# Scoring the last three groups a group ahead, and mixing two quarters directly, in a fused attention and two-FFN kernel

## The chip, the cores and the metric

The kernel runs on one core of a Trainium2 chip. The metric is the device time of one execution in microseconds, as the median of several runs. The engines are TensorE (PE; its weight loads are shown as PEld), VectorE (DVE), ScalarE (ACT), GpSimd (POOL) and SyncE (SP), which here only issues DMAs. Each engine takes its instructions in the order in which the program lists them.

## The reference

12480 tokens of 128 numbers attend to 32 inducing points, and the result goes through two feed-forward layers of width 2048.

```python
def mab(q, kv):
    s = scale * (q @ kv.transpose(0, 2, 1))
    s = s - s.max(-1, keepdims=True)
    a = np.exp(s)
    a /= a.sum(-1, keepdims=True) + 1e-09
    return a @ kv
h = mab(I, x)                      # 32 points attend to 12480 tokens
y = mab(x, h)                      # 12480 tokens attend to 32 points
# first layer
u = y @ w_in
y = (u * np.clip(u + 3.0, 0.0, 6.0) / 6.0) @ w_out
# second layer
r = np.maximum(y @ w_in2, 0.0)
out = (r * r) @ w_out2
```

The four weight matrices are float64 in memory, read as 64-bit words and turned into float32 on the chip.

## The kernel before

**The first pass** (lines 420 to 442) computes `h`. The tokens come in eight groups (`GROUPS`, of 2, 4, 4, 4, 4, 3, 2 and 2 blocks, each block four times 128 or 48 tokens). For group g, `scores` makes the 32 scores of each token on TensorE (L339, 256, 304 or 512 columns) and their running maximum on VectorE (L343); `exps` makes the exponentials on ScalarE (L349); `turn_x` transposes the tokens (L359) and copies them out (ScalarE, L364); `turn_e` transposes the exponentials (L372) and copies them out (VectorE, L374, and L377 for a block of 48); `accumulate` multiplies the two (L384, copy L388). In iteration g, group g is scored and its tokens are turned, while the exponentials of group g-1 are turned and accumulated. The scores use two PSUM buffers, the transposes four, the exponentials two. After the last group, `common_max` and `weigh` (L393 to L417) weigh the groups against each other, and lines 443 to 466 sum them and divide, which gives `ht4`, four copies of the transposed `h`.

**Weights are converted beside it.** A matrix is handled in quarters, a0 to a3 for the first up projection, b for its down projection, c and d for the second layer. A quarter has three steps: `first_stage` (ScalarE L179; VectorE L187, L191), `second_stage` (VectorE L200, L208) and `third_stage` (an add on GpSimd, L220). `tick()` puts the steps of `EARLY` between the others: tick 8 and 9 belong to iteration 4, 10 and 11 to iteration 5, and so on. `third_stage` of a quarter frees its load buffer, and once all loads of `LOADS` are out it also issues the next loads, c0 first (L156); the first to do so is that of b1, in `beside(-1, ...)` ahead of the main loop.

**Loads** are issued by SyncE in the order of `LOADS`: x is a group of tokens, a and b are quarters, n is the copy of the last group that needs no transpose.

**Mixing.** The tokens' second attention and the first up projection are merged: `a_t` (attention weights, `att_turn`, L641) times `m4`, where `m4` is `h` times the first weight matrix, as a high and a low part. `m4` has 128 rows: two copies of the 32 high rows and two of the low ones. Quarter 0 of its columns is made directly from `ht4` (`mix`, L484, 128 rows at once; `mix_high`, L490; `mix_low`, L494). Quarters 1 to 3 are made for 32 rows each (`mix_rest`, L501), split by `rest_high` (L516) and `rest_low` (L522), and spread to their rows by DMAs (`spread_rest`, L509, 64 KB each). `fill` issues transposes whose result nobody reads.

**The main loop** (k = 0 to 199 and a tail) runs `up1(k)` (L679, two matmuls of quarter k // 2 for the first eight k), `gate1(k)` (ScalarE L687, VectorE L688), `down1(k - 2)` (L715) and, 11 steps later, the second layer. The PSUM tag `h` has three buffers that `ps`, `rest`, `pt`, `h1` and `h2` take in turn; `y` and `o` have one each. The second block of 512 tokens gets its attention weights from `att_scores(1)` at k = 2 to `att_turn(1)` at k = 5, where the tile `pt` is written.

Of the kernel before, what the change touches and what calls it, by code (L numbers as in the profile page):

```python
# [30 lines left out]
KEPT = 5  # L31
TURN_V = {}
NATURAL = {7}


LOADS = [("x", 0), ("x", 1), ("x", 2), ("a", 0), ("x", 3), ("a", 1), ("x", 4), ("a", 2), ("a", 3),
         ("x", 5), ("b", 0), ("x", 6), ("x", 7), ("b", 1), ("n", 7), ("b", 2), ("b", 3)]

# [30 lines left out]
def induced_attention_then_two_ffn(  # L71
# [185 lines left out]
    def fill(n, pool, tag, bufs):  # L257
        t = pool.tile([P, P], F32, tag=tag, name="fill", bufs=bufs)
        for i in range(n):
            nc.tensor.transpose(t, ident, ident)  # L260
# [3 lines left out]
    def tick():  # L264
        ticks.append(len(ticks))
        return jobs(EARLY.get(ticks[-1], ""))
# [3 lines left out]
    def load_until(item):  # L270
        while item in todo:
            load(todo.pop(0))
# [9 lines left out]
    with ExitStack() as pro:  # L282
# [52 lines left out]
        def scores(g):  # L335
            n = run[g]
            s1[g] = pps.tile([P, n], F32, tag="s1", name="s1", bufs=2)
            for j in range(J):
                nc.tensor.matmul(  # L339
                    s1[g][M * j:M * (j + 1), :], lhsT=inds, rhs=xg[g][:, j * n:(j + 1) * n],  # L340
                    start=True, stop=True,
                )
            nc.vector.tensor_reduce(  # L343
                out=nmax[:, g:g + 1], in_=s1[g], axis=AX.X, op=ALU.max, negate=True
            )

        def exps(g):
            es[g] = pp.tile([P, run[g]], F32, tag="es", name="es", bufs=2)
            nc.scalar.activation(  # L349
                es[g], s1[g], AF.Exp, bias=nmax[:, g:g + 1], scale=1.0,  # L350
                accum_out=lsum[:, g:g + 1],
            )
# [13 lines left out]
        def turn_e(g):  # L366
            nb = len(GROUPS[g])
            t = pps.tile([P, nb, P], F32, tag="xt", name="ett", bufs=4)
            et[g] = pp.tile([P, nb, P], F32, tag="et", name="et", bufs=2)
            for b, blk in enumerate(GROUPS[g]):  # L370
                o = sum(GROUPS[g][:b])
                nc.tensor.transpose(t[:blk, b, :], es[g][:, o:o + blk], ident)  # L372
            whole_blocks = sum(blk == P for blk in GROUPS[g])
            nc.vector.tensor_copy(et[g][:, :whole_blocks], t[:, :whole_blocks])  # L374
            for b in range(whole_blocks, nb):
                blk = GROUPS[g][b]
                nc.vector.tensor_copy(et[g][:blk, b], t[:blk, b])  # L377

        def accumulate(g):
            nb = len(GROUPS[g])  # L380
            acc = hacc[g % 2][:, g // 2, :]
            for b, blk in enumerate(GROUPS[g]):
                for j in range(J):
                    nc.tensor.matmul(  # L384
                        acc[M * j:M * (j + 1), :], lhsT=et[g][:blk, b, M * j:M * (j + 1)],
                        rhs=xn[g][:blk, j * nb + b, :], start=(b == 0), stop=(b == nb - 1),
                    )
            nc.scalar.copy(hsb[:, g, :], acc)  # L388


        def common_max():
            nmin = pp.tile([P, 1], F32, name="nmin")
            nc.vector.tensor_reduce(out=nmin, in_=nmax, axis=AX.X, op=ALU.min)  # L393
            nm4 = pp.tile([P, J], F32, name="nm4")
            nc.vector.tensor_scalar_mul(nm4, blk4, nmin)
            return nm4
# [23 lines left out]
        for g in range(NG):  # L420
            load_until(("x", min(g + 3, NG - 1)))
            load_until(("n", g))
            scores(g)
            if g:
                turn_e(g - 1)
            if g == NG - 1:
                load_until(todo[-1] if todo else None)
                nm4 = common_max()
            for b in range(len(GROUPS[g])):
                if g not in NATURAL:  # L430
                    turn_x(g, b)
                if b == 0:
                    exps(g)
            tick()
            if g:
                accumulate(g - 1)
            tick()
        turn_e(NG - 1)
        rw, rl = weigh(nm4)
        accumulate(NG - 1)  # L440
        tick()

        pg = pps.tile([P, D], F32, tag="xt", name="pg", bufs=4)
        for g in range(NG - 1):
# [4 lines left out]
            )  # L449
        hg = pp.tile([P, D], F32, tag="sel4", name="hg")  # L450
        nc.scalar.copy(hg, pg)
        pl = pps.tile([P, M], F32, tag="s1", name="pl", bufs=2)
        nc.tensor.matmul(pl, lhsT=ones, rhs=rl, start=True, stop=True)
        ph = pps.tile([P, M], F32, tag="xt", name="ph", bufs=4)
# [25 lines left out]
    mixed = {}  # L480

    def mix(q):
        mixed[q] = ap_.tile([P, CW], F32, tag="o", name="mixed")
        nc.tensor.matmul(  # L484
            mixed[q], lhsT=ht4.rearrange("p j i -> p (j i)"), rhs=whole.pop(("a", q)),
            start=True, stop=True,
        )

    def mix_high(q):
        nc.scalar.copy(m4[:, q * CW:(q + 1) * CW], mixed[q])  # L490
# [6 lines left out]

    def mix_rest():
        rest["m"] = hp.tile([P, CW], F32, tag="h", name="rest")
        for q in range(1, J):  # L500
            nc.tensor.matmul(  # L501
                rest["m"][M * (q - 1):M * q, :], lhsT=ht4[:, 0, :], rhs=whole.pop(("a", q)),
                start=True, stop=True,
            )

    def spread_rest(part, groups):
        for q in range(1, J):
            for i in groups:
                nc.sync.dma_start(  # L509
                    m4[M * i:M * (i + 1), q * CW:(q + 1) * CW].bitcast(F32),  # L510
                    part[M * (q - 1):M * q, :].bitcast(F32),
                )

    def rest_high():
        rest["h"] = ep.tile([P, CW], F32R, tag="hi1", name="resthigh")
        nc.scalar.copy(rest["h"][:M * (J - 1), :], rest["m"][:M * (J - 1), :])  # L516
        spread_rest(rest["h"], (0, 1))

    def rest_low():
        n = M * (J - 1)  # L520
        t = ep.tile([P, CW], F32R, tag="lo1", name="restlow")
        nc.vector.tensor_tensor(  # L522
            out=t[:n, :], in0=rest["m"][:n, :], in1=rest["h"][:n, :], op=ALU.subtract
        )
        spread_rest(t, (2, 3))
# [91 lines left out]
    def att_norm(c):  # L617
        a = att_weights(c)
        att[c] = a
        if c < TURNS:  # L620
            a4 = sp.tile([P, J, 2, 2, M], F32R, tag="a4", name="a4", bufs=1)
            nc.vector.tensor_copy(a4[:, :, 0, 0, :], a)
            nc.scalar.copy(a4[:, :, 1, 0, :], a)
            for u in range(2):
                nc.vector.tensor_tensor(
                    out=a4[:, :, u, 1, :], in0=a, in1=a4[:, :, 0, 0, :], op=ALU.subtract
                )
            att[c] = a4
            return a4[:, 0, 1, 1, :1].bitcast(F32)
        return a[:, 0, :1]  # L630
# [201 lines left out]
    mix(0)  # L832
    att_exp(0)
    mix_high(0)
    mix_rest()
    fill(8, ap_, "y", 1)
    att_norm(0)
    rest_high()
    att_turn(0)
    fill(3, ap_, "y", 1)  # L840
    mix_low(0)
    rest_low()
    merge(("b", 1))
    tick()
    beside(-1, tick())
# [1 line left out]
    for k in range(K + OFF + L2 + 1):  # L847
        c, p = divmod(k, NP)
        j = k - OFF

        if k == NP + L1 - 1:
            on(down1, k - L1)
        on(up1, k)
        on(gate1, k)
        if k < 2:
            fill(8, ap_, "o", 1)
        on(square2, j - 1)
        on(up2, j)
        on(relu2, j)
        on(high2, j - 1)  # L860
        on(low2, j - 2)
        on(low1, k - 1)
        if k != NP + L1 - 1:
            on(down1, k - L1)
        on(down2, j - L2)
        last = g1[k][:, 0, :1] if k < N1 else lo1[k - 1][:, 0, :1].bitcast(F32) if N1 < k < K else None
        last = jobs(LATER.get(k, "")) or last
        if c + 1 < NCH:
            for chunks in BATCHES[1:]:
                if p == 1 and c + 2 == chunks[0]:  # L870
                    load_x(chunks[:2])
                    load_x(chunks[2:])
            stage = p - 2 if c == 0 else p
            if stage == 0:
                att_scores(c + 1)
                last = att_shift(c + 1)
            if stage == 1:
                att_exp(c + 1)
            if stage == 2:
                last = att_norm(c + 1)  # L880
            if stage == 3:
                if c + 1 < TURNS:
                    att_turn(c + 1)
                else:
                    last = att_spread(c + 1)
        beside(k, last)
        on(high1, k)
# [28 lines left out]
```

## Time and profile before

| | us |
|---|---|
| median of 3 runs | 959.04 |
| lowest and highest run | 958.35, 960.85 |
| the profiled execution | 958.2 |
| its span, first to last instruction | 956.4 |

The page gives for each engine its busy time, its share of the span and its number of instructions. In the timeline a row is a run of like instructions of one engine: start, duration, engine, line, operation, written and read tiles, shapes, count, and in brackets how long the engine was idle before it and what ended that. `SPq` rows are the issuing of DMAs. The durations of matmuls are modelled and overlap.

### The profile page before, as it was taken

The page shows a single profiled execution, that of the slowest core. Times are in us where ns is not written, and L with a number is a line of the kernel's source. Part 1 is how long each engine was busy: PE and PEld are TensorE (multiplying, and loading weights), DVE is VectorE, ACT ScalarE, POOL GpSimd, SP SyncE. Part 2 cuts the span into 40 slices and gives each one's busy share as a digit, 9 for nine tenths or more (in the row PEclk, how much of TensorE's full clock was granted, in tenths as well). Part 3 has the DMA queues.
Part 4 walks back from the last instruction along what each step waited for, and adds up shares of the span by engine and source line. Part 5 has one row for each costly group of instructions (what it writes and reads, how often), then busy time and mean ns, then how long its engine had stood idle before and what let it go on. Part 6 is the DMA issues. An engine that isn't in the chain of part 4 may idle for free.

```text
span 956.4 us, 12916 instructions
## 1 busy us (share of the span) xinstructions
PE 944.8 (99%) x4617; PEld 767.1 (80%) x4617; DVE 794.2 (83%) x969; ACT 812.3 (85%) x925; POOL 248.6 (26%) x412
## 2 busy tenths in 40 slices
PE   9899999999999999999999999999999999999998
PEld 7546678888888888888888888888888888888898
DVE  5887788888888888888888888888888888888774
ACT  6568888888888888888888888888888888889887
POOL 1233222222222222222222222222222222222222
PEclk9999999999999999999999999999999999999999
DMA  9451000001000000100000100010000100000000
GB/s 365 150 184 56 7 18 23 2 21 38 31 22 18 5 23 16 52 23 10 14 23 9 47 23 8 17 56 6 18 23 4 45 23 3 21 20 2 17 13 15
DMA packets 31247, 35.07 MB, mean 37 GB/s; under 512 B 7632, under 2 KB 24272, under 8 KB 30672
## 3 DMA queue, kind: packets, MB, share of 16 engines
q1 hardware_dynamic: 31184, 34.25, 10.9%
q8 instruction: 36, 0.59, 0.2%
q14 instruction: 27, 0.22, 0.1%
HBM read 21.18 MB, written 6.39 MB: 29 GB/s over the span
## 4 chain that ended last, share of the span: by engine, by line
PE 95%; DVE 2%; DMA 1%; ACT 0%; SPq 0%; issue 0%; DVEq 0%; ACTq 0%
PE h L756 28%; PE oacc L727 27%; PE yacc L727 26%; PE h L679 9%; PE yacc L715 2%; PE oacc L715 1%; PE ps L543 1%; DMA xg<-in_xT 1%; PE xt L359 1%; DMA raw<-in_w2a 0%; PE s L339 0%; PE hacc L384 0%; SPq L509 0%; DVE cve L191 0%; DVE et L374 0%
## 5 line engine op out<-in xcount | busy, mean ns | idle before, releaser
L688 DVE SCALAR_TENSOR_TENSOR g<-g,h 128x1024 f32<-128x1024 f32 (+2 forms) x200 | 238.7, 1193 | 119.2 <-ACT g L687 116.7
L687 ACT ACTIVATE g<-h,small 128x1024 f32<-128x1024 f32 (+2 forms) x200 | 219.1, 1096 | 114.4 <-PE h L679 114.1
L791 DVE TENSOR_TENSOR lo<-g,hi 128x1024 fp32r<-128x1024 f32 (+3 forms) x193 | 229.3, 1189 | 7.8 <-PE oacc L727 4.1
L707 DVE TENSOR_TENSOR lo<-g,hi 128x1024 fp32r<-128x1024 f32 (+2 forms) x184 | 219.4, 1192 | 0.8 <-POOL hi L699 0.8
L771 ACT ACTIVATE g<-g 128x1024 f32<-128x1024 f32 (+3 forms) x201 | 206.0, 1025 | 0.2
L767 ACT ACTIVATE g<-h 128x1024 f32<-128x1024 f32 (+3 forms) x201 | 199.2, 992 | 3.3 <-PE h L756 2.1
L783 ACT CAST hi<-g 128x1024 fp32r<-128x1024 f32 (+1 forms) x186 | 191.7, 1031 | 0.0
L699 POOL TENSOR_SCALAR hi<-g 128x1024 fp32r<-128x1024 f32 (+2 forms) x182 | 187.3, 1029 | 0.4 <-DMA at<-al 0.2
L756 PE MATMUL h<-yh,wl 128*128 128x512 f32 (+2 forms) x400 | 153.7, 384 | 0.0
L756 PE MATMUL h<-yh,wh 128*128 128x512 f32 (+2 forms) x400 | 153.7, 384 | 0.0
L756 PE MATMUL h<-yl,wh 128*128 128x512 f32 (+2 forms) x400 | 153.7, 384 | 0.0
L679 PE MATMUL h<-at,m 128*128 128x512 f32 (+2 forms) x400 | 129.0, 404 | 2.5 <-DMA m<-restlow 2.1
L727 PE MATMUL oacc<-hi,wh 128*128 128x512 f32 (+2 forms) x384 | 116.5, 384 | 0.0
L727 PE MATMUL oacc<-hi,wl 128*128 128x512 f32 (+2 forms) x384 | 116.4, 384 | 0.0
L727 PE MATMUL oacc<-lo,wh 128*128 128x512 f32 (+2 forms) x384 | 116.4, 384 | 0.0
L826 POOL COPY small<-lo 128x1 f32<-128x1 f32 x115 | 21.7, 189 | 344.5 <-DVE lo L707 344.5
L727 PE MATMUL yacc<-hi,wl 128*128 128x512 f32 (+2 forms) x368 | 111.2, 383 | 0.0
L727 PE MATMUL yacc<-hi,wh 128*128 128x512 f32 (+2 forms) x368 | 111.2, 383 | 0.0
L727 PE MATMUL yacc<-lo,wh 128*128 128x512 f32 (+2 forms) x368 | 111.2, 383 | 0.0
L679 PEld LDWEIGHTS h<-at,m 128*128 128x128 f32 x400 | 74.3, 188 | 26.0 <-issue 8.5
L756 PEld LDWEIGHTS h<-yl,wh 128*128 128x128 f32 x400 | 75.1, 188 | 14.5
L756 PEld LDWEIGHTS h<-yh,wh 128*128 128x128 f32 x400 | 75.1, 188 | 14.2
(125 smaller groups left out, 915.5 us busy)
## 6 DMA issues: line engine op xcount, KB each, us to landing
outT<-osb SPq DMA_DIRECT2D x23, 256.0 KB, 2.2
xc<-in_xT SPq DMA_DIRECT2D x9, 512.0 KB, 4.6
xg<-in_xT SPq DMA_DIRECT2D x4, 1024.0 KB, 7.2
at<-ah SPq DMA_DIRECT2D x168, 16.0 KB, 1.8
at<-al SPq DMA_DIRECT2D x168, 16.0 KB, 1.8
raw<-in_w1a SPq DMA_DIRECT2D x4, 512.0 KB, 8.7
raw<-in_w1b SPq DMA_DIRECT2D x4, 512.0 KB, 7.1
raw<-in_w2a SPq DMA_DIRECT2D x4, 512.0 KB, 6.3
```

The source lines that it names most:

```text
L679: nc.tensor.matmul(h1[k][:, u, :size[c]], lhsT=m4[:, f * P:(f + 1) * P], rhs=a_t[c], start=True, stop=True)
L687: nc.scalar.activation(g1[k], h, AF.Relu, bias=three)
L688: nc.vector.scalar_tensor_tensor(out=g1[k], in0=g1[k], scalar=6.0, in1=h, op0=ALU.min, op1=ALU.mult)
L699: nc.gpsimd.tensor_scalar(out=hi1[k], in0=g1[k], scalar1=1.0, scalar2=1.0, op0=ALU.mult, op1=ALU.mult)
L707: nc.vector.tensor_tensor(out=lo1[k], in0=g1.pop(k), in1=hi1[k], op=ALU.subtract)
L715: nc.tensor.matmul(acc, lhsT=w[:, f * P:(f + 1) * P], rhs=g[:, u, :], start=(p == 0 and u == 0), stop=(p == NP - 1 and u == 1),)
L727: nc.tensor.matmul(acc, lhsT=w[:, f * P:(f + 1) * P], rhs=g[:, u, :], start=(p == 0 and n == 0), stop=(p == NP - 1 and n == 5),)
L756: nc.tensor.matmul(h2[k][:, u, :size[c]], lhsT=w, rhs=y, start=(n == 0), stop=(n == 2))
L767: nc.scalar.activation(g2[k][:, u, :], h[:, u, :n], AF.Relu)
L771: nc.scalar.activation(g2[k][:, u, :], g2[k][:, u, :], AF.Square)
L783: nc.scalar.copy(hi2[k][:, u, :], g2[k][:, u, :])
L791: nc.vector.tensor_tensor(out=lo2[k][:, u, :], in0=g[:, u, :], in1=hi2[k][:, u, :], op=ALU.subtract)
```

## The change

The order of the first pass is changed for groups 5, 6 and 7. They are scored, and their exponentials made, at the end of the iteration before theirs, behind `turn_x` of that iteration and ahead of its first tick. In the last iteration, which then has no scores, `common_max` comes first, the exponentials of groups 6 and 7 are turned one behind the other, `weigh` follows, and two fill transposes stand ahead of `accumulate(6)`. The tick with the first step of b1 comes after the copy `hg`. In `LOADS`, x5 goes ahead of a3 and x6 ahead of b0.

In the mixing, quarters 0 and 1 are made directly (`mix(1)` in the PSUM buffer `y`), and quarters 2 and 3 go through `mix_rest` and the DMAs, of which there are now four for the high part and four for the low. Eight fill transposes go. `rest_high` moves behind the low parts of the direct quarters, and `rest_low` moves into the main loop, behind `gate1(0)`.

```diff
@@ -31,10 +31,11 @@
 KEPT = 5
 TURN_V = {}
 NATURAL = {7}
-
-
-LOADS = [("x", 0), ("x", 1), ("x", 2), ("a", 0), ("x", 3), ("a", 1), ("x", 4), ("a", 2), ("a", 3),
-         ("x", 5), ("b", 0), ("x", 6), ("x", 7), ("b", 1), ("n", 7), ("b", 2), ("b", 3)]
+AHEAD = 5
+
+
+LOADS = [("x", 0), ("x", 1), ("x", 2), ("a", 0), ("x", 3), ("a", 1), ("x", 4), ("a", 2), ("x", 5),
+         ("a", 3), ("x", 6), ("b", 0), ("x", 7), ("b", 1), ("n", 7), ("b", 2), ("b", 3)]
 
 
 
@@ -420,25 +421,31 @@
         for g in range(NG):
             load_until(("x", min(g + 3, NG - 1)))
             load_until(("n", g))
-            scores(g)
+            if g < AHEAD:
+                scores(g)
+            if g == NG - 1:
+                load_until(todo[-1] if todo else None)
+                nm4 = common_max()
             if g:
                 turn_e(g - 1)
             if g == NG - 1:
-                load_until(todo[-1] if todo else None)
-                nm4 = common_max()
+                turn_e(g)
+                rw, rl = weigh(nm4)
             for b in range(len(GROUPS[g])):
                 if g not in NATURAL:
                     turn_x(g, b)
-                if b == 0:
+                if b == 0 and g < AHEAD:
                     exps(g)
+            if AHEAD <= g + 1 < NG:
+                scores(g + 1)
+                exps(g + 1)
             tick()
             if g:
+                if g == NG - 1:
+                    fill(2, pps, "xt", 4)
                 accumulate(g - 1)
             tick()
-        turn_e(NG - 1)
-        rw, rl = weigh(nm4)
         accumulate(NG - 1)
-        tick()
 
         pg = pps.tile([P, D], F32, tag="xt", name="pg", bufs=4)
         for g in range(NG - 1):
@@ -449,6 +456,7 @@
             )
         hg = pp.tile([P, D], F32, tag="sel4", name="hg")
         nc.scalar.copy(hg, pg)
+        tick()
         pl = pps.tile([P, M], F32, tag="s1", name="pl", bufs=2)
         nc.tensor.matmul(pl, lhsT=ones, rhs=rl, start=True, stop=True)
         ph = pps.tile([P, M], F32, tag="xt", name="ph", bufs=4)
@@ -480,7 +488,7 @@
     mixed = {}
 
     def mix(q):
-        mixed[q] = ap_.tile([P, CW], F32, tag="o", name="mixed")
+        mixed[q] = ap_.tile([P, CW], F32, tag="y" if q else "o", name="mixed")
         nc.tensor.matmul(
             mixed[q], lhsT=ht4.rearrange("p j i -> p (j i)"), rhs=whole.pop(("a", q)),
             start=True, stop=True,
@@ -497,27 +505,27 @@
 
     def mix_rest():
         rest["m"] = hp.tile([P, CW], F32, tag="h", name="rest")
-        for q in range(1, J):
+        for q in range(2, J):
             nc.tensor.matmul(
-                rest["m"][M * (q - 1):M * q, :], lhsT=ht4[:, 0, :], rhs=whole.pop(("a", q)),
+                rest["m"][M * (q - 2):M * (q - 1), :], lhsT=ht4[:, 0, :], rhs=whole.pop(("a", q)),
                 start=True, stop=True,
             )
 
     def spread_rest(part, groups):
-        for q in range(1, J):
+        for q in range(2, J):
             for i in groups:
                 nc.sync.dma_start(
                     m4[M * i:M * (i + 1), q * CW:(q + 1) * CW].bitcast(F32),
-                    part[M * (q - 1):M * q, :].bitcast(F32),
+                    part[M * (q - 2):M * (q - 1), :].bitcast(F32),
                 )
 
     def rest_high():
         rest["h"] = ep.tile([P, CW], F32R, tag="hi1", name="resthigh")
-        nc.scalar.copy(rest["h"][:M * (J - 1), :], rest["m"][:M * (J - 1), :])
+        nc.scalar.copy(rest["h"][:M * (J - 2), :], rest["m"][:M * (J - 2), :])
         spread_rest(rest["h"], (0, 1))
 
     def rest_low():
-        n = M * (J - 1)
+        n = M * (J - 2)
         t = ep.tile([P, CW], F32R, tag="lo1", name="restlow")
         nc.vector.tensor_tensor(
             out=t[:n, :], in0=rest["m"][:n, :], in1=rest["h"][:n, :], op=ALU.subtract
@@ -832,14 +840,15 @@
     mix(0)
     att_exp(0)
     mix_high(0)
+    mix(1)
     mix_rest()
-    fill(8, ap_, "y", 1)
     att_norm(0)
+    mix_high(1)
+    att_turn(0)
+    mix_low(0)
+    mix_low(1)
+    fill(3, ap_, "o", 1)
     rest_high()
-    att_turn(0)
-    fill(3, ap_, "y", 1)
-    mix_low(0)
-    rest_low()
     merge(("b", 1))
     tick()
     beside(-1, tick())
@@ -852,6 +861,8 @@
             on(down1, k - L1)
         on(up1, k)
         on(gate1, k)
+        if k == 0:
+            rest_low()
         if k < 2:
             fill(8, ap_, "o", 1)
         on(square2, j - 1)
```

## Rows read from the trace of the kernel before

**Rows 1.** The page, first part: busy us, share of the span, instructions.

```profile
PE 944.8 (99%) x4617; PEld 767.1 (80%) x4617; DVE 794.2 (83%) x969; ACT 812.3 (85%) x925; POOL 248.6 (26%) x412
```

**Rows 2.** Waits of TensorE from 58 us on: us in total, times, longest us.

```profile
PE pt L641 <- DVE a L625: 1.2, 1, 1.2
PE yacc L715 <- DVE yl L745: 0.5, 1, 0.5
```

**Rows 3.** Timeline 22 to 36 us, TensorE: transposes of group 4, scores of group 5.

```profile
21.82 1.04 PE L359 MATMUL xt<-ident,xg 128*128 128x128 f32 x8
...
23.68 0.69 PE L339 MATMUL s<-xlast,row 128*32 128x304 f32 x8
```

**Rows 4.** The same timeline, VectorE.

```profile
21.80 0.58 DVE L187 TENSOR_SCALAR cve<-raw 128x512 uint32<-128x512 uint32 x1
...
25.13 0.68 DVE L374 COPY et<-ett 128x512 f32<-128x512 f32 x1
...
25.73 0.85 DVE L200 TENSOR_SCALAR cve<-cve 128x512 uint32<-128x512 uint32 x1
...
26.61 0.69 DVE L208 SCALAR_TENSOR_TENSOR cve<-raw,cve 128x512 uint32<-128x512 uint32 x1
...
27.22 0.42 DVE L187 TENSOR_SCALAR cve<-raw 128x512 uint32<-128x512 uint32 x1
...
27.68 1.40 DVE L191 TENSOR_SCALAR cve<-cve 128x512 f32<-128x512 f32 x1
...
31.43 0.42 DVE L343 TENSOR_REDUCE kept<-s 128x1 f32<-128x256 f32 x1 [0.43 <-PE s L339]
...
33.30 0.42 DVE L374 COPY et<-ett 128x256 f32<-128x256 f32 x1 [0.77 <-PE ett L372]
```

**Rows 5.** The same timeline, GpSimd.

```profile
25.02 1.27 POOL L220 TENSOR_TENSOR wa<-cve,cva 128x512 int32<-128x512 int32 x1 [2.92 <-ACT cva L179]
...
27.45 1.34 POOL L220 TENSOR_TENSOR wa<-cve,cva 128x512 int32<-128x512 int32 x1 [1.16 <-DVE cve L208]
```

**Rows 6.** DMA issues at 12.04, 47.93 and 48.56 us: count, KB, us to landing.

```profile
xlast<-in_xT SPq DMA_DIRECT2D x1, 608.0 KB, 10.5
raw<-in_w2a SPq DMA_DIRECT2D x1, 512.0 KB, 4.5
m<-restlow SPq DMA_DIRECT2D x1, 64.0 KB, 3.5
```

**Rows 7.** Windows of 2 us: busy us (count) by engine, PEclk, DMA share, GB/s.

```profile
14.00:16.00 2.00, 2.00 (x45) 1.24 (x42) 1.39 (x3) 2.00 (x6) 0.00 (x0) 1.00 1.06 432
46.00:48.00 2.00, 0.53 (x2) 0.48 (x3) 1.97 (x4) 0.00 (x0) 1.12 (x3) 1.00 0.43 109
54.00:56.00 2.00, 2.00 (x7) 0.97 (x6) 1.06 (x2) 1.03 (x2) 0.00 (x0) 1.00 0.95 307
```

**Rows 8.** Timeline 36 to 66 us, all engines.

```profile
41.67 0.69 DVE L522 TENSOR_TENSOR restlow<-rest,resthigh 96x512 fp32r<-96x512 f32 x1
...
44.29 1.03 PE L260 MATMUL fill<-ident 128*128 128x128 f32 x8
...
44.82 3.70 SPq L509 DMA_DIRECT2D m<-restlow  x6
44.86 1.21 DVE L688 SCALAR_TENSOR_TENSOR g<-g,h 128x1024 f32<-128x1024 f32 x1
...
47.47 0.70 PE L679 MATMUL h<-at,m 128*128 128x512 f32 x2 [2.14 <-DMA m<-restlow]
...
48.56 2.83 SPq L156 DMA_DIRECT2D raw<-in_w2a  x4
...
53.13 0.69 ACT L179 ACTIVATE cva<-raw 128x512 int32<-128x512 uint32 x1 [1.07 <-DMA raw<-in_w2a]
...
55.06 1.22 DVE L688 SCALAR_TENSOR_TENSOR g<-g,h 128x1024 f32<-128x1024 f32 x1 [0.94 <-ACT g L687]
...
58.15 0.63 PE L641 MATMUL pt<-ident_r,a 128*128 128x128 f32 x4 [1.16 <-DVE a L625]
```

## The prediction

> **What bounds the kernel now.** I read the page first: TensorE is busy 99% of the span [rows 1], so a stage is worth what it makes TensorE wait. Then the waits of TensorE after 58 us: there are two, 1.2 and 0.5 us long, and none later [rows 2]. From the first of them, at 58.15, to the end TensorE has work all the time; what the change does before that point moves the end by the same amount, and what it does to loads, VectorE or ScalarE afterwards is worth nothing unless it makes a new wait. So the question is when that matmul (`pt` of `att_turn(1)`) can start. I went through the stretch before it in the timeline, engine by engine, in program order, since every engine takes its instructions in the order in which they are written.
>
> In the last part of the first pass VectorE is the full engine: it carries the conversion of the weights (`EARLY`) besides the maxima and the copies of the turned exponentials, and from 21.80 to 33.30 it is idle for only 0.43 and 0.77 us [rows 4]. Three of its conversion steps are longer than their kind: L187 0.58, L200 0.85 and L191 1.40 where 0.42 to 0.43 is usual [rows 4]. Each began while GpSimd ran an L220 add of 1.27 us, and each ended about 0.3 after the add did: the add from 27.45 to 28.79 and L191 to 29.08 [rows 4, 5]. So these one-input steps wait until a running add is almost over, here until 0.14 before its end. The Trainium skill says the same of the mechanism (SBUF — State Buffer, Who interferes with whom): whichever of the two has the shared pair of ports first keeps it for the whole instruction.
>
> **The change, first pass.** The groups 0 to 4 keep their order. In iteration 4, `scores(5)` now comes behind `turn_x(4)`, and its maximum stands on VectorE's queue ahead of tick 8, that is ahead of the conversion of a2 that VectorE could start at 21.80 [rows 4]. The transposes end at 22.86; the scores of 304 columns take 0.69 [rows 3]; so the maximum can't begin before 23.55. Input group 5 is no obstacle: it landed 10.5 after 12.04, at 22.5 [rows 6], and now goes one 512 KB load earlier, 1.2 us at the 432 GB/s of that stretch [rows 7]. Behind the waiting maximum stand the conversions, behind these `et` of group 4, and for that waits `accumulate(4)`.
>
> I lay the queue of VectorE out again, from start to start as in rows 4: L187 to L191 0.46, L208 to the next 0.61, `et` 0.60, a maximum 0.4 (0.42 is the row). Maximum 23.55; a2's first two steps from 23.95; its second two from 24.87, the last ending at 26.03. That end releases the add of a2 on GpSimd 0.15 later, as 27.30 released 27.45 [rows 4, 5]; ScalarE's part of a2 (0.69 for this step, [rows 8]) follows the exponential of group 5 and is over by 25.7, so the add runs from 26.18 to 27.45. a3's L187 starts at 25.94, ahead of it, but L191 meets it and ends near 27.75: the same phase as in the row of 1.40. Then `et` 4 at 27.67 (25.13 before), maximum 6 at 28.27, a3's second two at 28.60, b0's L187 at 29.67; its L191 meets the add of a3, as before, and ends at 31.46; `et` 5 31.38, maximum 7 31.92, b0's second two 32.26, the common maximum 33.33, `et` 6 33.71, `et` 7 34.05. Before it is 33.30. As an account: 1.75 new idle ahead of maximum 5 and 0.5 more of collision (0.97 on L191 for 0.42 on L200), less 0.15 of the first collision and less the two waits of 0.43 and 0.77, is +0.9. I take **+0.8**, between the two ways. All scores and exponentials come off the path, but the path was VectorE's. TensorE is done with its part early (`accumulate(4)` waits some 1.6 us for `et`), and the steps from `et` 7 to the mixed weights stay one chain, so they move by the same 0.8. `fill(2)`, the tick behind `hg` and the two softmax steps that move up cost nothing here: VectorE's queue is in the same order from `nall` to `ht4`. ScalarE and the later loads (`n7` waits for `accumulate(4)`, so 1.9 later, and is needed last) have room.
>
> Bounds of this term: without the collision of a2 it is 0.8 - 0.95 = -0.15. Upwards, `nm4` (L395, a one-input step as well) starts within 0.1 of the add of b0; behind it it would cost up to 1.2 more.
>
> **The change, mixing** (times of before; the 0.8 comes on top). Removed: `fill(8)`, about 1.03 [rows 8], and quarter 1 from the spread rows. Added: `mix(1)`, a pair of matmuls in the place of that fill, a copy and a 0.69 subtraction in the place of `rest_high` and `rest_low`. Up to `up1(0)` each engine has as much to do as before: no gain, no loss. But `rest_low` now stands behind `gate1(0)` on VectorE, and `up1(1)` needs the third PSUM buffer of `h`, which `rest` holds until `rest_low` has read it (`ps`, `rest`, `pt`, `h1(0)`, `h1(1)` take three buffers in turn). The first gate starts at 44.86 and gives way after 1.13; so `rest_low` runs 45.99 to 46.68 (0.69), where it ran at 41.67 [rows 8]. `up1(1)` then starts at 46.75, then 0.7 for it and 1.03 for the fill behind it, and `up1(2)` at 48.45 instead of 47.47. The wait for the spread rows, 2.14 us [rows 8], is gone and a wait for `rest_low` with a fill behind it takes its place.
>
> From 47.47 TensorE worked without a break until 57.0 (it is full in every slice as in 54 to 56, [rows 7]) and waited 1.16 for `pt` [rows 8]. One us later it is through at 58.0, still before 58.15. On VectorE the gates of k = 1 to 3 come 1.0 to 1.6 later, the last of them at 53.1; c0's first conversion no longer waits for its load (ScalarE sat idle 1.07 for it, and the gate at 55.06 sat 0.94 behind that, [rows 8]), because on SyncE's queue c0 to c3 now go ahead of the four spreads of `rest_low`. `rest_high` is done at about 42.9, behind the copy of `at` that lets `up1(0)` start; its four spreads at 0.62 each (six took 3.70) end at 45.4, and the loads start there instead of at 48.56 [rows 8]. `up1(4)` is ready at 53.45, its gate at 55.28 instead of 55.06: +0.2 for `pt`.
>
> What the trace of before does not show is the time at which these four spreads land behind 2 MB of loads. They are issued from 48.2, behind four loads that took 2.83 to issue [rows 8]. If the loads go at 432 GB/s (1.2 us each) the rows of quarter 2 are there at about 53.4, and nothing waits; at the pace of the same tensors before, 307 GB/s, 1.7 us each [rows 7], they land at about 55.7, and `pt` is at +2.5. A load alone of the queue's front took 4.5 from issue to landing, and a spread beside it 3.5 [rows 6]. Less than nothing is excluded, but for 0.15, by TensorE's own work. I take **+0.5**, nearer the low end, as the loads meet little else.
>
> **Sum.** +0.8 + 0.5 = +1.3. The profiled execution took 958.2 (span 956.4), so 959.5 for such a one; the median of the runs is 0.84 above it, 959.04, and the forecast is **960.3**.
>
> **Rivals.** (1) The collision doesn't come about, because VectorE's L191 gets in first or the add starts later: -0.15 + 0.2, so 959.1. For it: the two are 0.2 apart. Against: before, a step in just this phase was stopped. 0.17. (2) The slower side: the spreads of `rest_low` land behind c3, on the path of `up1(4)`. Price 0.8 + 2.5 = 3.3, so 962.3; it decides from a landing of quarter 2 later than 53.45, and takes the total over 0.3% from about 55.3. For it the 307 GB/s and the 3.5 us; against it that small spreads may pass between the loads. 0.13. (3) `nm4` behind the add of b0: 0.8 + 1.2 + 0.5, so 961.5. 0.12. (4) TensorE's clock falls in the longer gap before `up1(1)`, about 2.7 us where it was 2.1. Against: the granted clock stayed at 1.00, the level of 2.4 GHz, in the slice in which it worked 0.53 of 2.00 us [rows 7]. With half of the clock the fill and the pair of matmuls behind the gap, 1.7 us, take 3.4: 960.3 + 1.7 = 962.0. 0.05. The Trainium skill (TensorE: Matmul & The Clock Gate, What's actually happening) has a gate that halves the clock when the engine is idle and gives it back after activity; no run here shows one that fell. (5) The change does what it says and VectorE is not in the way (it takes the conversions while it would wait): the pass gains its 1.2 of waits and `up1(2)` its 1.0: 956.8. Against: the written order is the order in every row. 0.03. The forecast itself, +0.7 to +2.0: 0.50.
>
> About 0.3%, 2.9 us, is what a measurement can tell from no change. Slower by that: most of (2), a part of (3) and (4) where they add to a late landing, 0.10; faster: 0.02; within: 0.88. The range holds the forecast, (1), (3) and most of (2): 958.2 to 962.6.
>
> **What would show it.** Right: VectorE idle about 1.7 us before the maximum of group 5; an L191 of about 1.4 behind the add of a2; `et` 7 near 34.0; the second `up1` released by `restlow`; `up1(2)` 1.8 later than now; ScalarE not waiting for `in_w2a` any more. Wrong: `et` 4 before 26.5, or `pt` before 58. If TensorE waits for a spread of `restlow` at `up1(4)`, it is rival 2; a granted clock under 1.00 is rival 4.

## The result and the profile after

The changed kernel took 966.17 us (median of six runs, 965.45 at best) against 959.47 for the kernel before: a ratio of 1.0074, with a 95% interval of 1.0060 to 1.0088. It is 6.7 us slower, and the forecast of 960.3, with its range up to 962.6, was wrong. The profiled execution of the changed kernel took 966.46, with a span of 964.7 against 956.4. In this profile the lines of the code are one to eight further down (L191 is L192, L395 is L396, L522 is L530, L679 is L687).

From 58.15 to the end the kernel before kept TensorE at work, but for 0.5 us [rows 2]; so does the new one from the same matmul on. The waits of TensorE after 58 us in the changed kernel, as in rows 2:

```profile
PE h L687 <- DMA m<-restlow: 6.1, 1, 6.1
PE yacc L723 <- DVE yl L753: 0.5, 1, 0.5
```

`pt` of `att_turn(1)` starts at 66.21 where it started at 58.15 [rows 8], which is 8.06 of the 8.3 us in the span. So the loss is ahead of it, and there is a wait of 6.1 us that was not there before. The first pass in the changed kernel, timeline from 20 to 36 us:

```profile
22.97 0.72 PE L340 MATMUL s<-xlast,row 128*32 128x304 f32 x8
...
23.75 0.47 DVE L344 TENSOR_REDUCE kept<-s 128x1 f32<-128x304 f32 x1 [1.69 <-PE s L340]
...
26.36 1.32 POOL L221 TENSOR_TENSOR wa<-cve,cva 128x512 int32<-128x512 int32 x1 [4.09 <-ACT cva L180]
...
26.59 1.38 DVE L192 TENSOR_SCALAR cve<-cve 128x512 f32<-128x512 f32 x1
27.89 0.68 DVE L375 COPY et<-ett 128x512 f32<-128x512 f32 x1
...
30.33 1.39 DVE L192 TENSOR_SCALAR cve<-cve 128x512 f32<-128x512 f32 x1
...
33.74 1.32 DVE L396 TENSOR_SCALAR nm<-small,nmin 128x4 f32<-128x4 f32 x1
33.78 1.26 POOL L221 TENSOR_TENSOR w<-cve,cva 128x512 int32<-128x512 int32 x1 [2.35 <-DVE nmin L394]
34.98 0.74 DVE L375 COPY et<-ett 128x256 f32<-128x256 f32 x2
35.12 0.39 PE L401 MATMUL pm<-nm,sel 128*128 128x4 f32 x2 [1.39 <-DVE nm L396]
```

VectorE waits 1.69 us for the scores of group 5; two L192 steps take 1.38 and 1.39 because an add of GpSimd is running; and `nm4`, four numbers wide, takes 1.32, where it took 0.23 before; the add of b0 is recorded 0.04 behind it. That this add is the cause is tested below. The two copies of groups 6 and 7 end at 35.72; that of group 7 ended at 33.72 before [rows 4], 2.0 earlier. The mixing and the start of the main loop follow, with the row of `ht4` in the kernel before ahead of them:

```profile
36.52 0.29 DVE L463 TENSOR_TENSOR ht<-ph,rec 128x128 f32<-128x128 f32 x1
```

The changed kernel:

```profile
38.52 0.29 DVE L471 TENSOR_TENSOR ht<-ph,rec 128x128 f32<-128x128 f32 x1
...
45.73 0.70 PE L687 MATMUL h<-at,m 128*128 128x512 f32 x2
...
47.36 2.91 SPq L157 DMA_DIRECT2D raw<-in_w2a  x4
48.11 0.68 DVE L530 TENSOR_TENSOR restlow<-rest,resthigh 64x512 fp32r<-64x512 f32 x1
...
48.24 0.73 PE L687 MATMUL h<-at,m 128*128 128x512 f32 x2 [0.93 <-DVE g L696]
...
50.36 2.80 SPq L517 DMA_DIRECT2D m<-restlow  x4
...
51.55 1.88 PE L723 MATMUL yacc<-g,w 128*128 128x512 f32 x4
...
59.52 1.19 PE L687 MATMUL h<-at,m 128*128 128x512 f32 x2 [6.09 <-DMA m<-restlow]
...
60.51 3.62 PE L723 MATMUL yacc<-g,w 128*128 128x512 f32 x4
...
66.21 0.96 PE L649 MATMUL pt<-ident_r,a 128*128 128x128 f32 x4
```

`ht4` is 2.0 later than before (36.52). `up1(2)`, which waited 2.14 for spread rows [rows 8], now waits 0.93 for the first gate and starts at 48.24, only 0.8 later than before: 1.2 of the 2.0 are won back. Then `up1(4)` is ready at about 53.4, where the four matmuls from 51.55 end, and waits 6.09 for the spreads of `rest_low`. SyncE issued these from 50.36, behind the four loads of the second layer's weights. DMA issues from 47 to 55 us, with the median time to landing in the last column:

```profile
raw<-in_w2a SPq DMA_DIRECT2D x4, 512.0 KB, 6.3
...
m<-restlow SPq DMA_DIRECT2D x4, 64.0 KB, 8.0
```

A spread of 64 KB took 8.0 us to land: the first of the four landed at 59.0, behind c3, which landed at 58.6. The Trainium skill says that an issuing engine's DMAs share one ring on each DMA engine, and that this takes its descriptors in order (DMA: Bandwidth & Descriptors, Queues, rings and completion order); the landings agree. And the `yacc` row above shows a second cost: four matmuls in 3.62 us, where four of the same kind took 1.88 at 51.55. Windows of 2 us (busy us and count by engine, PEclk, DMA share, GB/s):

```profile
56.00:58.00 2.00, 0.00 (x0) 0.00 (x0) 0.07 (x1) 0.00 (x0) 0.00 (x0) 1.00 1.09 214
58.00:60.00 2.00, 0.48 (x1) 0.50 (x2) 0.00 (x0) 0.00 (x0) 0.00 (x0) 0.54 1.09 315
60.00:62.00 2.00, 2.00 (x4) 1.00 (x3) 0.10 (x1) 1.11 (x1) 0.00 (x0) 0.50 0.34 118
62.00:64.00 2.00, 2.00 (x4) 0.76 (x3) 1.90 (x5) 0.00 (x0) 0.00 (x0) 0.50 0.00 0
64.00:66.00 2.00, 2.00 (x6) 1.27 (x5) 0.77 (x4) 1.28 (x2) 0.00 (x0) 0.75 0.00 0
66.00:68.00 2.00, 2.00 (x10) 1.25 (x9) 1.80 (x3) 1.43 (x4) 0.00 (x0) 1.00 0.00 0
```

Late in the wait the granted clock falls from 1.00 to 0.50, that is from 2.4 to 1.2 GHz, and with TensorE at work again it is back at 1.00 in the last of these windows. The Trainium skill has this gate (TensorE: Matmul & The Clock Gate, What's actually happening): throttled when idle, released by activity; this run agrees.

### The profile page after: what moved, and what is told of

It reads as the page before. It is cut to its first block, busy times and chain, and to the rows that moved or that the text cites. A ratio compares the mean times of both kernels' runs of the same rounds, so it can differ in the third digit from the quotient of the medians.

```text
span 964.7 us, 12894 instructions
## 1 busy us (share of the span) xinstructions
PE 948.4 (98%) x4611; PEld 768.4 (80%) x4611; DVE 795.6 (82%) x970; ACT 814.5 (84%) x926; POOL 248.9 (26%) x412
## 4 chain that ended last, share of the span: by engine, by line
PE 96%; DVE 2%; DMA 1%; issue 0%; ACT 0%; POOL 0%; SPq 0%; DVEq 0%; POOLq 0%
PE h L764 28%; PE oacc L735 26%; PE yacc L735 25%; PE h L687 9%; PE yacc L723 3%; PE oacc L723 1%; DMA m<-restlow 1%; PE xt L360 1%; PE ps L551 1%; PE s L340 1%; DVE cve L192 0%; PE fill L261 0%; PE hacc L385 0%; DVE g L696 0%; DVE cve L188 0%
## 5 line engine op out<-in xcount | busy, mean ns | idle before, releaser
L687 PE MATMUL h<-at,m 128*128 128x512 f32 (+2 forms) x400 | 130.0, 407 | 7.2 <-DMA m<-restlow 6.1
L687 PEld LDWEIGHTS h<-at,m 128*128 128x128 f32 x400 | 74.7, 189 | 31.6 <-issue 15.4
```

Of the source, the lines that this page charges most:

```text
L687: nc.tensor.matmul(h1[k][:, u, :size[c]], lhsT=m4[:, f * P:(f + 1) * P], rhs=a_t[c], start=True, stop=True)
```

## The experiments

Three theories. **A**: the loads c0 to c3, which the program now lists ahead of `rest_low`, hold back its spreads; TensorE waits, and the half clock follows from the wait. **B**: `rest_low` itself is too late on VectorE, and the loads don't matter. **C**: the loss is the first pass. Every ratio below is to the kernel before on the same chip.

**The loads behind the spreads.** `rest_low` stays where the change put it. `load_waiting` is the loop of `third_stage` that issues c0 to c3; it now does nothing as long as `ahead` holds it back.

```diff
+    ahead.append(len(waiting) - 0)
     beside(-1, tick())
...
         if k == 0:
             rest_low()
+            ahead.clear()
+            load_waiting()
```

> The changed kernel, but SyncE issues the loads c0 to c3 behind the four spreads of rest_low instead of ahead of them; rest_low itself stays behind the first gate. Theory A (the spreads stand behind 2 MB of loads, and the fall of the clock follows from the wait): the spreads are issued from 48.8 and land by 52, up1(4) doesn't wait for them, the granted clock stays at 1.00; c0 then lands near 56, some 2 us later than before the change, and ScalarE waits for it, so 962 (961 to 963.5). Theory B (rest_low comes too late on VectorE, the loads don't matter): the wait at up1(4) stays, 965 or more. Theory C (the loss is in the first pass): 965 or more, with no wait at up1(4).

963.49 us, ratio 1.0037 (1.0023 to 1.0051). TensorE no longer waits at `up1(4)`. The spreads land in 2.0 us (window 47 to 55 us, as above):

```profile
m<-restlow SPq DMA_DIRECT2D x4, 64.0 KB, 2.0
```

That is 8.0 against 2.0 with nothing changed but the order on one queue. B falls: the subtraction was as late as in the changed kernel. What was gained is partly lost again, as expected: c0 lands late, and `pt` waits 2.7 for VectorE, whose gate stood behind it (waits of TensorE, 36 to 75 us; each edit moves the line numbers again):

```profile
PE pt L656 <- DVE a L640: 2.7, 1, 2.7
```

In this profile the granted clock also fell twice, behind the wait for `nm4` (0.50 in the window from 36 to 38) and behind this wait (0.50 in the window from 64 to 66). So its time is not the price of the late c0 alone.

**Two loads ahead, two behind.**

> The changed kernel with half of the suspected cause: c0 and c1 are issued ahead of the spreads of rest_low, c2 and c3 behind them. Theory A: the spreads land behind c1, near 55 to 56, up1(4) waits some 2 us instead of 6.1, 962.5 (961.5 to 964). Theory B: the wait doesn't change, 965 or more. Theory C: 965 or more.

961.86 us, 1.0023 (1.0012 to 1.0034). The wait at `up1(4)` is 2.7 where four loads made it 6.1 and none made it nothing:

```profile
PE h L694 <- DMA m<-restlow: 2.7, 1, 2.7
```

and the clock stays at 1.00 behind it. The wait goes with the number of loads ahead.

**`rest_low` early**, ahead of the loads and of the first gate.

```diff
     rest_high()
+    rest_low()
     merge(("b", 1))
...
-        if k == 0:
-            rest_low()
```

> The changed kernel with rest_low directly behind rest_high, ahead of the merge of b1, so that its spreads are ahead of the loads and its subtraction ahead of the first gate. Theories A and B alike: no wait at up1(2) nor at up1(4), clock 1.00; what is left is the first pass (ht4 2.0 later) less some 0.7 to 1.2 in the mixing: 960.5 (959.5 to 961.5). Theory C: 964 or more.

960.41 us, 1.0006 (0.9995 to 1.0017), as expected of A and B alike. C falls as the main cause: the new first pass is all in there.

**The parts alone.** The first pass of the change with the old mixing, and the new mixing with the old first pass.

> The first pass of the change alone (with its order of loads), the mixing as before the change. Theories A and B: ht4 some 1.8 to 2.0 later, of which 1.1 is nm4 behind the add of b0 and the rest VectorE's idle time ahead of the maximum of group 5; everything behind it moves along: 961.4 (960.8 to 962). Theory C: 964 to 966.

> The mixing of the change alone (two quarters direct, rest_low behind the first gate, so the loads ahead of its spreads), with the first pass and the order of loads as before. Theory A: the wait at up1(4) of some 6 us and the half clock behind it are there without the new first pass; 966.2 less the 2 to 2.7 that the pass alone cost: 964 (963 to 965). Theory C (first pass): 960 or less.

The pass alone took 961.87, 1.0027 (1.0016 to 1.0038); the mixing alone 964.09, 1.0046 (1.0030 to 1.0062). 2.7 and 4.3 make up the whole (7.0 for 6.7). In the mixing alone `up1(4)` waits 6.55 and the clock falls to 0.50:

```profile
58.18 1.19 PE L679 MATMUL h<-at,m 128*128 128x512 f32 x2 [6.55 <-DMA m<-restlow]
```

**The clock by itself.** 46 fill transposes ahead of `up1(4)` keep TensorE at work while it waits.

```diff
+        if k == 4:
+            fill(46, ap_, "o", 1)
         on(up1, k)
```

> The changed kernel with 46 fill transposes ahead of up1(4), which keep TensorE at work during the wait for the spreads (46 by 0.13 is 5.9 us against 6.09). Theory A: the spreads land as late as before, near 59.4, but the granted clock stays at 1.00 and TensorE does the matmuls behind the wait at full speed; the chain by up1(4), its gate and pt then takes some 5 us for 6.7: 964.5 (963.8 to 965.2). If the clock costs nothing behind a wait like this: 966.2, as without the fills.

965.13 us, 1.0060 (1.0039 to 1.0081). Timeline, 52 to 68 us:

```profile
60.01 0.70 PE L687 MATMUL h<-at,m 128*128 128x512 f32 x2 [0.49 <-DMA m<-restlow]
60.55 1.88 PE L723 MATMUL yacc<-g,w 128*128 128x512 f32 x4
...
64.99 0.63 PE L649 MATMUL pt<-ident_r,a 128*128 128x128 f32 x4 [0.38 <-DVE a L633]
```

From `up1(4)` to `pt` it takes 4.98 instead of 6.69: the half clock cost 1.7 us. The spreads land no sooner. Only 1.0 of this is in the medians, and the intervals of the two kernels overlap, so the 1.7 rests on the two profiles. In this profile the clock fell in another place, at the wait for `nm4` in the first pass, as it did in that of `rest_low` early. Windows of the run with the fills:

```profile
34.00:36.00 2.00, 1.09 (x8) 0.77 (x11) 1.67 (x4) 0.27 (x1) 0.83 (x1) 0.70 1.12 405
36.00:38.00 2.00, 2.00 (x41) 1.86 (x43) 1.66 (x6) 0.34 (x3) 0.00 (x0) 0.50 0.49 188
```

There `ht4` is at 39.60, 1.1 later than in the changed kernel's profile, where the clock held through the same wait.

**`nm4` ahead of the add.** The first pass alone, with the add of b0 made to wait for `nm4`.

```diff
-    ... 13: "b0.3" ...
+    ... 14: "b0.3" ...
...
+                nc.gpsimd.tensor_copy(turn, nm4[:, :1])
                 rw, rl = weigh(nm4)
```

> The first pass alone (as in e4_pass_only), but the add of b0 on GpSimd is made to wait for nm4 by a copy of one column ahead of it. Theory A: nm4 takes 0.2 to 0.25 instead of 1.32, ht4 is 1.1 earlier, the gap of TensorE ahead of it is 0.3 instead of 1.4: 960.7 (960.0 to 961.2). If the add isn't what nm4 waited for: 961.9, as e4_pass_only.

959.43 us, 0.9994 (0.9985 to 1.0003): 2.4 better than the pass alone, and more than expected. `nm4` is short, but there is a second difference (timeline, 28 to 36 us):

```profile
31.35 2.63 SPq L157 DMA_DIRECT2D raw<-in_w2a  x3
33.69 0.23 DVE L396 TENSOR_SCALAR nm<-small,nmin 128x4 f32<-128x4 f32 x1
```

By tick 14 all first loads are out, so the helper of the moved add also issued c0 to c2, some 19 us earlier than in the pass alone. The edit did two things, so I took them apart.

> As e7_pass_nm (first pass alone, the add of b0 behind nm4), with the loads c0 to c3 held back to the place where e4_pass_only issues them, since moving the add had also issued three of them earlier. If nm4 alone is worth 1.1: 960.7 (960.1 to 961.3). If the 2.4 between e4_pass_only and e7_pass_nm came from the earlier loads: 961.9.

With the loads held back: 960.83, 1.0010 (0.9999 to 1.0022). By the medians about 1.0 of the 2.4 is `nm4` and about 1.4 the loads; by the ratios, each to the kernel before on its own chip, it is about 1.6 and 1.5. The interval of this run overlaps with both others, so the sizes are rough. But `nm4` falls from 1.32 to 0.23 in both, and `pt` waits 2.3 with the loads held back and 0.4 without. The share of the loads holds a fall of the clock too: behind the wait at `pt` it is at 0.50 with the loads held back (first row), and at 1.00 without (second row; windows of 2 us).

```profile
62.00:64.00 2.00, 2.00 (x3) 0.67 (x2) 1.97 (x4) 2.00 (x3) 0.43 (x2) 0.50 0.00 0
62.00:64.00 2.00, 2.00 (x7) 1.14 (x6) 1.97 (x4) 1.64 (x3) 1.12 (x2) 1.00 0.58 170
```

**The loads early, in the changed kernel and in the one before.** Only the entry of b0's add is moved by one tick.

> The changed kernel, with one entry of the list of conversion steps moved: the add of b0 from tick 13 to tick 14. By then all first loads are out, so that add's helper issues c0 to c2 some 15 us earlier, on a free queue; only c3 is left ahead of the spreads of rest_low. Nothing else is mended (nm4 still meets the add, rest_low stays behind the first gate). Theory A: the spreads land at about 53, up1(4) waits for them by 0.5 at most, the clock stays: 960.2 (959.2 to 961.2). Theory B (rest_low too late on VectorE): 964 or more.

> The kernel before the change, with only the add of b0 at tick 14, which issues c0 to c2 some 15 us earlier. If the wait of 1.16 at pt was due to the load of c0 (ScalarE sat idle 1.07 for it): 958.6 (957.9 to 959.2). If pt has other work behind it in time: 959.5, no change.

In the changed kernel: 960.02, 1.0002 (0.9989 to 1.0014). Moving one entry takes back the 6 us; `up1(4)` waits 0.5:

```profile
55.30 0.70 PE L687 MATMUL h<-at,m 128*128 128x512 f32 x2 [0.54 <-DVE nm L594]
```

The row names a step of VectorE that ended at 55.14; the second spread of `rest_low` landed at 55.10, and `up1(4)` started 0.20 behind it, as it did in the run with two loads ahead (56.31 and 56.51). So I count this wait as one for the spreads; the row alone does not show it.

In the kernel before: 959.13, 0.9986 (0.9975 to 0.9996), a gain of about 0.1%, near the upper end of what was expected; `pt` waits 0.4 instead of 1.2. Five of its twelve executions took 957.5 to 957.8, with a mean granted clock of 0.999 or 1.000, and seven 959.1 to 959.4, with 0.998.

**All mended.** `rest_low` early, the add behind `nm4` (with the early loads that this brings), and tick 8 ahead of the scores of group 5.

```diff
+            if g == AHEAD - 1:
+                tick()
             if AHEAD <= g + 1 < NG:
                 scores(g + 1)
                 exps(g + 1)
-            tick()
+            if g != AHEAD - 1:
+                tick()
```

> Both parts of the change with the three causes mended: rest_low directly behind rest_high, so its spreads go ahead of the loads; the add of b0 behind nm4; and tick 8 (a2's first conversion steps) ahead of the scores of group 5, so that VectorE has work while it would wait for them. Theory A: against e3_low_early's 960.4 a gain of 1.1 for nm4 and of 0.9 for the idle time: 958.4 (957.5 to 959.3). If VectorE's idle time in the pass wasn't on the path: 959.3.

958.00 us (957.82 to 958.22), 0.9979 (0.9970 to 0.9988): faster than both kernels, and 0.2% faster than the one before. VectorE's wait for the scores of group 5 is down from 1.69 to 0.74, and TensorE's for `nm4` from 1.39 to 0.30:

```profile
23.80 0.47 DVE L344 TENSOR_REDUCE kept<-s 128x1 f32<-128x304 f32 x1 [0.74 <-PE s L340]
...
33.15 0.38 PE L401 MATMUL pm<-nm,sel 128*128 128x4 f32 x2 [0.30 <-DVE nm L396]
```

What the change itself is worth, once mended, this does not show. The early loads alone gave the kernel before 0.1%, and the two intervals overlap; `pt` starts at 58.13 here, at 58.15 in the kernel before and at 57.45 in that with the early loads (the profiles). The two also differ in the clock: all eleven executions had a mean granted clock of 0.999 or 1.000, while of the 20 executions of the kernel before that the ratio is taken from one alone had this, at 958.66; the others had 0.996 to 0.998.

**Without the collisions.** The conversion steps of a3 and b0 a tick later.

```diff
-    ... 9: "a2.2 a3.1", 10: "a2.3 a3.2", 11: "a3.3 b0.1", 12: "b0.2", 14: "b0.3"
+    ... 9: "a2.2", 10: "a2.3 a3.1", 11: "a3.2", 12: "a3.3 b0.1", 13: "b0.2", 14: "b0.3"
```

> As f1_combined, with the conversion steps of a3, b0 one tick later, so that behind the step that releases an add on GpSimd VectorE has the copy of the exponentials and a maximum to do, not a one-input step. Theory A: each of the two steps of 1.39 falls to 0.8 at most, the copies of groups 4 and 5 come 1 to 1.8 earlier, ht4 1.0 to 1.5 earlier: 956.9 (956.2 to 957.8). If the collisions cost nothing on the path: 958.0.

959.13 us, 0.9992 (0.9981 to 1.0004): not better than 958.00, and expected was 956.9. Four of the twelve executions took 958.1 to 958.4, with a mean granted clock of 1.000, and eight 959.1 or more, with 0.998 or less. The collisions do go (no L192 is over 0.43 us, one L188 takes 0.92) and the copies of groups 4 and 5 come 1.7 and 1.2 us earlier. But `nm4` does not: the conversions still stand ahead of it on VectorE, and TensorE, done earlier, waits for it in one piece. Timeline and windows of this run:

```profile
33.37 0.39 PE L401 MATMUL pm<-nm,sel 128*128 128x4 f32 x2 [1.74 <-DVE nm L396]
```

```profile
32.00:34.00 2.00, 0.64 (x4) 0.48 (x4) 1.93 (x7) 0.00 (x0) 0.63 (x2) 0.92 1.09 387
34.00:36.00 2.00, 2.00 (x38) 1.71 (x40) 1.53 (x7) 0.57 (x2) 0.78 (x1) 0.50 1.05 409
```

The clock falls behind that wait, and `ht4` is at 38.09 instead of 36.79. Small waits, one to a group, became one large one, and in this profile the large one cost the clock.

## Why the prediction was wrong

**The path: right.** The end moved with `pt` (8.06 of 8.3), and nothing behind it mattered. Shown by the profile.

**VectorE ahead of group 5: right.** 1.69 us of idle time for 1.75, the maximum at 23.75 for 23.55, an L192 of 1.38 behind the add of a2, `et` 4 at 27.89 for 27.67. All of it is 0.2 late, since the whole pass started 0.2 later in this execution.

**`nm4`: the wrong case was taken.** The term was given as +0.8, with up to 1.2 more if `nm4` were held up by the add of b0 (rival 3, 0.12). It was: `nm4` was recorded as starting 0.04 ahead of the add and still took 1.32, so `ht4` moved by 2.0 and not by 0.8. With the add held back it took 0.23. The step that failed: a lead of 0.05 (33.51 for `nm4` and 33.56 for the add, by the prediction's own layout) was counted as a lead. L188 had a lead of 0.23 on the add of a2 (26.13 to 26.36) and did go first. The rule that whichever has the ports first keeps them (the Trainium skill, SBUF — State Buffer, Who interferes with whom) agrees with L192; for `nm4` the recorded starts do not show who had them first.

**`up1(1)` behind `rest_low`: wrong, and to the good.** I had the three buffers of `h` taken in turn, as the description of the kernel says too, so that `h1(1)` had to wait for `rest`. It started at 45.73, before `rest_low` (48.11). `up1(2)` started when the first gate had read `h1(0)` (0.93 of wait), before `rest_low` was over. So the buffer of `rest`, still in use, must have been passed over. `up1(2)` came 1.2 us earlier than it would have by `ht4` alone, not 1.0 later.

**The landing of the spreads: right mechanism, wrong size, and here the prediction was lost.** Rival 2 named it: the spreads of `rest_low` behind c0 to c3, at `up1(4)`. I gave it 0.13 and, at its worst, a landing at 55.7 in the times of before, 57.7 with the 2.0; it was 59.4. In the prediction the loads start at 45.4, at 1.2 to 1.7 us each, and the rows are there 8.0 to 10.3 later. Measured it was 12.0 (47.36 to 59.38, the second spread). From the first issue to the landing of c3 it took 11.2, and in the run with the loads behind the spreads 8.2: there c1 to c3 landed 1.2 to 1.4 apart, in the changed kernel c2 and c3 landed 2.3 and 2.1 behind the one before. c0 alone took 5.5 (4.5 before, [rows 6]) while the spreads of `rest_high` were under way. The row of a spread with 3.5 us beside a load [rows 6] was in hand, and I read it as a bound, not as a sign that the two slow each other. And from that range I took nearly the low end, +0.5 at `pt`; this term came out at +6.06, beside the +2.0 of `ht4`. Shown by the runs: with four loads ahead the wait is 6.1, with two 2.7, with one 0.5, with none nothing. That the two kinds slow each other is argued from these landings, not measured by itself.

**The clock: named, but in the wrong place.** Rival 4 had the fall in the gap ahead of `up1(1)`, with 1.7 us for one fill and one pair of matmuls. That gap did not come about. The fall came behind the wait for the spreads, and cost 1.7 there (the profile of the fills), over all the work from `up1(4)` to `pt`; that the two figures are equal is luck. I had the rivals as alternatives; but a late landing makes the gap in which the clock falls, so here rival 2 brought a fall of the clock with it. The price of rival 2, 3.3, was worked out without one.

The sum as it came out: `ht4` +2.0; -1.2 at `up1(2)`; +0.6 between `up1(2)` and the point where `up1(4)` is ready, which is the modelled end of the matmuls ahead of it (in the kernel before `up1(4)` started 0.6 ahead of that end); +6.1 for the wait; +1.7 for the clock; -1.2, as `pt` had waited that long before. That is +8.0 at `pt`, for 8.06 measured. Against the prediction's own worst landing, which put `pt` at 60.65, or 62.65 with the 2.0 of `ht4`, the 66.21 is 3.6 later: 1.7 by the landing and 1.7 by the clock make up nearly all of it.

## What to carry to other kernels

When a step with a DMA is moved down the program, list what the new place puts ahead of it on the issuing queue; here a helper that frees a buffer issued 2 MB of loads in between, and four small transfers paid for it. Prices of waits are not independent of each other: a wait of a few us on TensorE is to be priced with and without a fall of the clock behind it, and removing several small waits can make one large one. An edit of one list entry can do two things, and two runs are needed to see which of them paid.

## What the runs showed of the hardware

- A 64 KB transfer that landed 2.0 us after its issue with no load ahead of it took 8.0 (median of four) behind four loads of 512 KB issued in the 3 us before it.
- The granted clock fell from 1.00 to 0.50 in or behind waits of 6.1 and 6.6 us, behind waits of 1.9, 2.3 and 2.7 us at `pt` (the pass alone, the pass with the loads held back, the loads behind the spreads), and also behind a wait of 1.4 to 1.7 us in a stretch where TensorE had little to do, there in some executions only: the same wait of 1.39 left it at 1.00 in the changed kernel's profile and took it to 0.50 in that of the fills. It stayed at 1.00 behind 2.1 us at `up1(2)` in the kernel before and behind 2.7 at `up1(4)` with two loads ahead. What decides between the two the runs do not show.
- A step of VectorE four elements wide took 1.32 us where an add of GpSimd was recorded as starting 0.04 us behind it, and 0.23 with the add held back.
